# Lightning attention into a gated FFN: the first score matmuls of block n+2 moved behind the state update of block n+1

## The chip, the cores and the metric

The kernel runs on one core of a Trainium2 chip. The time is the device time of one execution in microseconds, over several runs; a separate execution is recorded by the profiler.

## What is computed

Two stages, one behind the other, on q, k, v of 4 batches, 8 heads, 768 positions and 64 features:

```python
# stage 1: linear attention with decay lam per head, block after block
intra = (qb @ kb.T * Dmask) @ vb            # within a block, lower triangle, lam ** (i - j)
inter = (qb * lam_pow) @ kv_state           # what earlier blocks left
out[block] = intra + inter
kv_state = lam_block * kv_state + (kb * rev_pow).T @ vb
# stage 2: x = out as (3072 tokens, 512), d_ff = 1536
y = (sigmoid(x @ w_gate) * (x @ w_val)) @ w_out
```

## The kernel before, in words

The sequence is cut into six blocks of 128 positions (`C = 128`, twice the reference's block; the decays are made for 128). Block n holds 128 positions of each of the four batches, so 512 tokens for the FFN. The order of the instructions on every engine is the order in which the program writes them (`tc.manual_schedule`): nothing is reordered, and each engine and each issuing queue goes through its own list.

For one block the pieces are:

- `load(n, "qkv", 0, B)` (L70 to L93): GpSimd (POOL) issues the loads of Q, K and V, cast to bf16.
- `transpose_by_dma(n)` (L225): SyncE (SP) issues two DMA transposes, Q into `QR` and K into `KR`, two buffers each. They wait for the loads.
- `t(n, bp)` (L268, `scale`, L242): VectorE (DVE) multiplies `QR` of a pair of batches by the decay into `QS`.
- `sc(n, bp)` and `m(n, bp)`: for each of the pair's two batches 8 score matmuls into two PSUM tiles `sp` (L299), and the masking multiplications `MT` on VectorE (L204), two for each batch.
- `a(n, 0, 1)` (`piece_a`, L316): 32 matmuls of `QS` with the state `Sb` (L324) and 32 of `MT` with V (L312) into four PSUM tiles `op`, one for each pair `bp` and `u`; four casts carry these into `XT[n]` (L339), the FFN's input.
- `c(n, 0, 1)` (L399): 32 matmuls of V with the decayed K (`kd`, made by POOL, L373) into two PSUM tiles `cp`; VectorE adds the faded old state `sd` (L382) into `Sb` (L406).
- `gv(n, ft)` (L410): 4 gate matmuls (`gp`, L415), a sigmoid on ScalarE (ACT, L418), 4 value matmuls (`vp`, L421), and the product `ht` on VectorE (L424), for each of 12 slices of d_ff.
- `piece_po(n, tt)` (L475): 12 matmuls with `WO` (L478), a copy on ScalarE (L481), and a store issued by SP (L486), for each of the four batches.

PSUM has eight buffers: five (`ps_at`, tag `ps`) go round among `op`, `sp` and the first `cp`; three (`ps_ff`, tag `ff`) go round among `gp`, `vp`, `po` and the second `cp`.

The loop from L638 on weaves block n's FFN with block nx = n+1's attention. In block n come, in this order: the transposes of nx; slices 0 and 1; fade, decayed K and the loads of n+2; slices 2 to 8; the scale of nx's first pair; slice 9; the scale of its second pair; slice 10; the scores of the first pair; slice 11; their second mask; then output matmuls of batch 0, scores of the second pair, outputs of batches 1 and 2, `a(nx)`, `c(nx)`, and outputs of batch 3. Ahead of the loop (L621 to L637) the same is written out for block 1's FFN and block 2's attention. Matmuls of the FFN use the whole 128\*128 array; the scores use it as 64\*128, `a` as 64\*64 and then 128\*64, and `c` as 128\*64.

Of the kernel before, what the change touches and what calls it, by code (L numbers as in the profile page):

```python
# [15 lines left out]
def kernel(  # L16
# [11 lines left out]
    nc = tc.nc  # L28
# [3 lines left out]
    NSTEP = S // C  # L32
# [144 lines left out]
    mask = const.tile([128, H, C], FP32, tag="mask")  # L177
# [22 lines left out]
    def masked(out, x, n, u):  # L200
        if n == 0:
            nc.vector.tensor_tensor(out=out, in0=x, in1=mask[:, u::2, :], op=ALU.mult)  # L202
            return
        nc.vector.tensor_tensor(  # L204
            out=out.rearrange("p (e x) c -> p e x c", e=2), in0=x.rearrange("p (e x) c -> p e x c", e=2),
            in1=mask.rearrange("p (x u e) c -> p u e x c", u=2, e=2)[:, u], op=ALU.mult)

    def half(e):
        return slice(e * 64, (e + 1) * 64)

    def head(g, u):
        return 4 * (g % 2) + 2 * u + g // 2
# [12 lines left out]
    def transpose_by_dma(n):  # L225
        QR[n] = trsb.tile([128, 2, B, 2, C], BF16, tag="QR", name="QR", bufs=2)
        kt = trsb.tile([128, 2, B, 2, C], BF16, tag="KR", name="KR", bufs=2)
        for dst, src in ((QR[n], Q[n]), (kt, K[n])):
            nc.sync.dma_start_transpose(out=dst.rearrange("p e b x c -> p (e b x) c"),
                                        in_=src.rearrange("p e b y d -> p (e b y d)"))  # L230
        for bp in range(NB2):
            KS[n, bp] = kt[:, :, 2 * bp:2 * bp + 2]
# [35 lines left out]
    def piece_t(n, bp):  # L268
        if n > 1 or bp == 1:
            scale(n, bp, QR[n][:, :, 2 * bp:2 * bp + 2] if n > 1 else HB["q"])  # L270
            return
        q1, k1 = (x[1][:, 0].rearrange("p (e b y d) -> p e b y d", e=2, b=2, y=HP) for x in (Q, K))
        tq = ps_at.tile([128, 2, 2, 2, C], BF16, name="tq", tag="ps")
        tk = ps_at.tile([128, 2, 2, 2, C], BF16, name="tk", tag="ps")

        def turn(out, x):
            for e in range(2):
                for i in range(2):
                    for g in range(2):
                        nc.tensor.transpose(out[:, e, i, g, :],  # L280
                                            x[:, e, i, 2 * g:2 * g + 2, :].rearrange("p y d -> p (y d)"), ident)

        turn(tq, q1)
        scale(n, bp, tq)
        turn(tk, k1)
        KS[n, bp] = trsb.tile([128, 2, 2, 2, C], BF16, tag="KS", name="KS")
        nc.scalar.copy(KS[n, bp], tk)
# [16 lines left out]
    def piece_m(n, b, us=(0, 1)):  # L304
        if us[0] == 0:
            MT[n, b] = mtp.tile([128, 2, HP, C], BF16, tag="MT", name="MT")
        for u in us:
            masked(MT[n, b][:, u], SP[n, b][u], n, u)

    def intra(n, b, out, m, start, stop):  # L310
        for e in range(2):
            nc.tensor.matmul(out[half(e)], lhsT=V[n][:, b, 2 * m + e, :],  # L312
                             rhs=MT[n, b][:, e, m, :] if n == 0 else MT[n, b][:, m % 2, 2 * e + m // 2, :],
                             start=start, stop=stop, skip_group_check=True)

    def piece_a(n, pairs):  # L316
        OP = {(bp, u): ps_at.tile([128, 2, 2, C], FP32, name="op", tag="ps")
              for bp in pairs for u in range(2)}
        for bp in pairs:
            for i in range(2):  # L320
                for x in range(2):
                    for u in range(2):
                        for e in range(2):
                            nc.tensor.matmul(OP[bp, u][half(e), x, i, :],  # L324
                                             lhsT=Sb[half(u), 2 * bp + i, 2 * e + x, :],
                                             rhs=QS[n, bp][half(u), e, i, x, :],
                                             start=(i == 0 and x == 0), stop=False,
                                             skip_group_check=True)
        for bp in pairs:
            for u in range(2):  # L330
                for i in range(2):
                    for x in range(2):
                        intra(n, 2 * bp + i, OP[bp, u][:, x, i, :], 2 * x + u, False, i == 1 and x == 1)
        if n not in XT:
            XT[n] = xtp.tile([128, NMT, B, C], BF16, tag="XT", name="XT")
        for bp in pairs:
            for u in range(2):
                cp = nc.vector.tensor_copy if n == 1 and bp == 0 and u else nc.scalar.copy
                cp(XT[n][:, u::2, 2 * bp:2 * bp + 2, :], OP[bp, u])  # L339

    def piece_a0(b, split=False):
# [44 lines left out]
    def kdh(n, b, h):  # L386
        if n == 1:
            return KD[n][:, b // 2].rearrange("p (e b y d) -> p e b y d", e=2, b=2, y=HP)[:, h % 2, b % 2, h // 2]
        return KD[n][:, b, h, :] if n == 0 else KD[n][:, h % 2, b, h // 2, :]

    def c(n, *pairs):
        for bp in pairs:
            pool, tag = (ps_at, "ps") if bp == 0 or n == 0 else (ps_ff, "ff")
            cp = pool.tile([128, 2, HP, D], FP32, name="cp", tag=tag)
            for i in range(2):
                for hp in range(HP):
                    for u in range(2):
                        h = head(hp, u)
                        nc.tensor.matmul(cp[half(u), i, hp, :], lhsT=kdh(n, 2 * bp + i, h),  # L399
                                         rhs=V[n][:, 2 * bp + i, h, :], start=(i == 0 and hp == 0),  # L400
                                         stop=(i == 1 and hp == HP - 1), skip_group_check=True)
            dst = Sb[:, 2 * bp:2 * bp + 2]
            if n == 0:
                nc.vector.tensor_copy(dst, cp)
            else:
                nc.vector.tensor_tensor(out=dst, in0=cp, in1=SD.pop(bp), op=ALU.add)  # L406
# [68 lines left out]
    def piece_po(n, tt):  # L475
        po = ps_ff.tile([128, DM], FP32, name="po", tag="ff")
        for ft in range(NFT):
            nc.tensor.matmul(po, lhsT=HT[n, ft][:, tt * 128:(tt + 1) * 128],  # L478
                             rhs=WO[:, ft, :], start=(ft == 0), stop=(ft == NFT - 1))
        ob = osb.tile([128, DM], FP32, tag="ob", name="ob")  # L480
        nc.scalar.copy(ob, po)  # L481
        parts = 2 if n == 0 and tt < 2 else 1
        rows = 128 // parts
        for i in range(parts):
            lo = tt * S + n * C + i * rows
            nc.sync.dma_start(out=out[lo:lo + rows, :], in_=ob[i * rows:(i + 1) * rows, :])  # L486
# [51 lines left out]
    def t(n, bp):  # L538
        piece_t(n, bp)

    def sc(n, bp):
        piece_s(n, [2 * bp, 2 * bp + 1])
        piece_m(n, 2 * bp)

    def m(n, bp):
        piece_m(n, 2 * bp + 1)

    def a(n, *pairs):
        piece_a(n, pairs)

    def gv(n, *fts):
        for ft in fts:
            piece_gv(n, ft)
# [39 lines left out]
    t(1, 0)  # L593
    gv(0, 9)
    sc(1, 0)
    m(1, 0)
    gv(0, 10)
# [11 lines left out]
    t(1, 1)  # L609
    gvh(1, 0, 6, 7)  # L610
    sc(1, 1)
    gvh(1, 0, 8)
    m(1, 1)
# [12 lines left out]
    t(2, 1)  # L626
    piece_po(0, 3)
    sc(2, 0)
    m(2, 0)
    piece_po(1, 0)  # L630
    sc(2, 1)
    m(2, 1)
    piece_po(1, 1)
    piece_po(1, 2)
    a(2, 0, 1)
    c(2, 0, 1)
    piece_po(1, 3)  # L637
    for n in range(2, NSTEP):  # L638
        nx = n + 1
        if nx == NSTEP:  # L640
            gv(n, *range(NFT))
            for tt in range(B - 1):
                piece_po(n, tt)
            piece_last(n, B - 1)
            break
        transpose_by_dma(nx)
        gv(n, 0, 1)
        if nx + 1 < NSTEP:
            fade()
            make_kd(nx)  # L650
            load(nx + 1, "qkv", 0, B)
        gv(n, 2, 3, 4, 5, 6, 7, 8)
        t(nx, 0)
        gv(n, 9)
        t(nx, 1)
        gv(n, 10)
        sc(nx, 0)
        gv(n, 11)
        m(nx, 0)
        piece_po(n, 0)  # L660
        sc(nx, 1)
        m(nx, 1)
        piece_po(n, 1)
        piece_po(n, 2)
        a(nx, 0, 1)
        if nx + 1 < NSTEP:
            c(nx, 0, 1)
        piece_po(n, 3)


# [28 lines left out]
```

## Time and profile before

| | |
|---|---|
| median of 3 runs | 226.52 us (226.45 to 226.9) |
| profiled execution | 226.60 us, of which the profiled span is 224.5 us |
| granted TensorE clock | 1.000 |
| TensorE matmuls busy | 218.5 us (97% of the span) |
| VectorE / ScalarE / GpSimd busy | 105.5 / 79.6 / 78.4 us |
| one block in the loop | 34.6 us (first gate matmul of blocks 2 and 3 at 87.1 and 121.7 us) |

The profile names an instruction by engine, line and tiles: "PE sp L299" is a score matmul. PE is TensorE's matmuls, PEld its weight loads; a row "sp<-QS,KR x16" is a group of 16. A time in a list of the timeline is the start from the beginning of the span, followed by the length. In the chain of work that ended last, a row starts where the one before it ends. Matmuls are pipelined and their ends are modelled, so the distance of two starts is the safer measure.

### The profile page before, as it was taken

How to read it: one execution, taken by the hardware profiler on the slowest of the kernel's cores; microseconds unless marked ns; L12 is line 12 of the kernel's file. 1: busy time of each engine (PE TensorE's matmuls, PEld its weight loads, DVE VectorE, ACT ScalarE, POOL GpSimd, SP SyncE). 2: the span in 40 equal slices, each digit the busy share in tenths (PEclk: the TensorE clock that was granted, in tenths of full speed). 3: DMA queues.
4: the chain of work that ended last, by engine and by line, in shares of the span. 5: the costliest groups of instructions: out<-in, count | busy, mean ns of one | idle time of the engine just before them, and what ended most of it. 6: DMA issues, size and time to landing. Idle time of an engine off the chain costs nothing.

```text
span 224.5 us, 4265 instructions
## 1 busy us (share of the span) xinstructions
PE 218.5 (97%) x1748; PEld 114.6 (51%) x1748; DVE 105.5 (47%) x192; ACT 79.6 (35%) x150; POOL 78.4 (35%) x77
## 2 busy tenths in 40 slices
PE   7799999999999999999999999999999999999994
PEld 2454455888854454444445444446444445444443
DVE  7796847595530713336732445742335840333300
ACT  5664334435422234333225333115333225333221
POOL 8995698983691008930006940000000000000000
PEclk9999999999999999999999999999999999999999
DMA  6999999999999992999021999021920012100022
GB/s 109 155 173 194 189 176 156 157 194 166 157 198 184 217 178 83 204 156 108 1 96 55 230 145 133 1 96 47 176 62 0 0 53 91 47 3 0 0 93 95
DMA packets 105891, 25.70 MB, mean 114 GB/s; under 512 B 96016, under 2 KB 102928, under 8 KB 105872
## 3 DMA queue, kind: packets, MB, share of 16 engines
q0 software_dynamic: 81264, 13.90, 80.0%
q1 hardware_dynamic: 23568, 11.28, 19.7%
q10 hardware_dynamic: 1040, 0.26, 0.5%
q8 instruction: 13, 0.21, 0.4%
q14 instruction: 6, 0.05, 0.1%
HBM read 28.32 MB, written 6.29 MB: 154 GB/s over the span
## 4 chain that ended last, share of the span: by engine, by line
PE 94%; DMA 3%; DVE 1%; issue 1%; ACT 1%; POOLq 0%
PE po L478 27%; PE gp L415 21%; PE vp L421 21%; PE gp L450 5%; PE gp L429 5%; PE vp L456 5%; PE op L312 3%; PE sp L299 3%; DMA kb<-in_k_dram 3%; PE op L324 1%; PE cp L399 1%; PE po L467 1%; DVE MT L202 1%; PE tk L238 0%; ACT XT L352 0%
## 5 line engine op out<-in xcount | busy, mean ns | idle before, releaser
L424 DVE TENSOR_TENSOR ht<-sg,vp 128x512 bf16<-128x512 bf16 x54 | 37.1, 687 | 64.0 <-PE vp L421 63.9
L478 PE MATMUL po<-WO,ht 128*128 128x512 bf16 x276 | 62.0, 380 | 0.0
L415 PE MATMUL gp<-XT,WG 128*128 128x512 bf16 x216 | 55.5, 380 | 0.0
L421 PE MATMUL vp<-XT,WV 128*128 128x512 bf16 x216 | 55.4, 379 | 0.0
L418 ACT ACTIVATE sg<-gp 128x512 bf16<-128x512 f32 x54 | 32.2, 597 | 59.0 <-PE gp L415 59.0
L478 PEld LDWEIGHTS <-ht 128*128 128x128 bf16 x276 | 26.3, 98 | 31.0
L421 PEld LDWEIGHTS <-WV 128*128 128x128 bf16 x216 | 21.1, 98 | 25.5
L415 PEld LDWEIGHTS <-WG 128*128 128x128 bf16 x216 | 20.8, 98 | 24.7
L481 ACT COPY ob<-po 128x512 f32<-128x512 f32 x23 | 13.5, 585 | 52.3 <-PE po L478 50.4
L204 DVE TENSOR_TENSOR MT<-sp,mask 128x512 bf16<-128x512 f32 x40 | 25.2, 683 | 10.1 <-PE sp L299 10.1
L382 POOL TENSOR_TENSOR sd<-Sb,dec 128x512 f32<-128x512 bf16 x8 | 8.1, 1037 | 42.0 <-DVE Sb L406 42.0
L450 PE MATMUL gp<-XT,WG 128*128 128x256 bf16 x96 | 14.4, 273 | 0.0
L456 PE MATMUL vp<-XT,WV 128*128 128x256 bf16 x96 | 14.4, 273 | 0.0
L460 DVE TENSOR_TENSOR ht<-sg,vp 128x256 bf16<-128x256 bf16 x24 | 10.0, 420 | 8.6 <-PE vp L456 8.6
L453 ACT ACTIVATE sg<-gp 128x256 bf16<-128x256 f32 x24 | 9.2, 383 | 13.0 <-PE gp L450 11.9
L91 POOL DMA_DIRECT2D vb<-in_v_dram x10 | 12.8, 1281 | 0.8 <-DMA WG<-in_moe_w_gate_dram 0.6
L373 POOL TENSOR_TENSOR kd<-kb,kds 128x1024 bf16<-128x1024 bf16 x6 | 11.3, 1904 | 4.1 <-DMA kb<-in_k_dram 4.1
L406 DVE TENSOR_TENSOR Sb<-cp,sd 128x512 bf16<-128x512 f32 x8 | 5.2, 686 | 15.4 <-PE cp L399 15.4
L339 ACT CAST XT<-op 128x512 bf16<-128x512 f32 x19 | 9.9, 598 | 2.1 <-PE op L312 2.0
L450 PEld LDWEIGHTS <-WG 128*128 128x128 bf16 x96 | 9.2, 98 | 1.8 <-issue 0.2
L456 PEld LDWEIGHTS <-WV 128*128 128x128 bf16 x96 | 9.4, 98 | 1.1
L77 POOL DMA_DIRECT2D qb<-in_q_dram x8 | 9.4, 1184 | 0.0
(79 smaller groups left out, 161.7 us busy)
## 6 DMA issues: line engine op xcount, KB each, us to landing
out_dram<-ob SPq DMA_DIRECT2D x21, 256.0 KB, 2.1
kb<-in_k_dram POOLq DMA_DIRECT2D x10, 256.0 KB, 8.7
qb<-in_q_dram POOLq DMA_DIRECT2D x8, 256.0 KB, 8.3
vb<-in_v_dram POOLq DMA_DIRECT2D x4, 512.0 KB, 13.2
WO<-in_moe_w_out_dram POOLq DMA_DIRECT2D x3, 512.0 KB, 8.6
WG<-in_moe_w_gate_dram POOLq DMA_DIRECT2D x5, 256.0 KB, 8.5
WV<-in_moe_w_val_dram POOLq DMA_DIRECT2D x5, 256.0 KB, 9.0
qb<-in_q_dram POOLq DMA_DIRECT2D x6, 128.0 KB, 8.3
```

The costliest lines, as they stand in the source:

```text
L91: nc.gpsimd.dma_start(out=lst[n][:, b0:b1], in_=src[b0:b1, :, sl, :].rearrange("b h s d -> s (b h) d"))
L204: nc.vector.tensor_tensor(out=out.rearrange("p (e x) c -> p e x c", e=2), in0=x.rearrange("p (e x) c -> p e x c", e=2), in1=mask.rearrange ...
L373: nc.gpsimd.tensor_tensor(out=KD[n][:, e], in0=K[n][:, e], in1=kds[:, e::2].unsqueeze(1).unsqueeze(3).to_broadcast([128, B, HP, D]), op=AL ...
L415: nc.tensor.matmul(gp, lhsT=WG[:, mt, fs], rhs=x[:, mt, :], start=(mt == 0), stop=(mt == NMT - 1))
L418: nc.scalar.activation(sg, gp, AF.Sigmoid)
L421: nc.tensor.matmul(vp, lhsT=WV[:, mt, fs], rhs=x[:, mt, :], start=(mt == 0), stop=(mt == NMT - 1))
L424: nc.vector.tensor_mul(HT[n, ft], sg, vp)
L429: nc.tensor.matmul(ps[:, lo:hi], lhsT=W[:, mt, ft * 128:(ft + 1) * 128], rhs=x[:, mt, lo:hi], start=(mt == 0), stop=(mt == NMT - 1))
L450: nc.tensor.matmul(gp[:, cs], lhsT=WG[:, mt, fs], rhs=x[:, mt, cs], start=(mt == 0), stop=(mt == NMT - 1))
L456: nc.tensor.matmul(vp[:, cs], lhsT=WV[:, mt, fs], rhs=x[:, mt, cs], start=(mt == 0), stop=(mt == NMT - 1))
L478: nc.tensor.matmul(po, lhsT=HT[n, ft][:, tt * 128:(tt + 1) * 128], rhs=WO[:, ft, :], start=(ft == 0), stop=(ft == NFT - 1))
L481: nc.scalar.copy(ob, po)
```

## The change

The scores of the first pair of batches (batches 0 and 1) of block n+2 are computed in block n, directly behind the state update `c` of block n+1, where they stood inside the next block's gate/value slices. What feeds them moves ahead with them: the two DMA transposes of block n+2 are issued behind slice 11 of block n in program order, and the scale of its first pair runs between the outputs of batches 1 and 2. Ahead of the loop the same is done for block 3. The scale of the second pair keeps its block and stands behind slice 8. The casts of `op` into `XT` with u = 1 go to VectorE for all blocks from 2 on; they were on ScalarE.

```diff
@@ piece_a
-                cp = nc.vector.tensor_copy if n == 1 and bp == 0 and u else nc.scalar.copy
+                cp = nc.vector.tensor_copy if u and (n > 1 or bp == 0) else nc.scalar.copy
                 cp(XT[n][:, u::2, 2 * bp:2 * bp + 2, :], OP[bp, u])
@@ ahead of the loop
     m(2, 0)
+    transpose_by_dma(3)
     piece_po(1, 0)
     sc(2, 1)
     m(2, 1)
     piece_po(1, 1)
+    t(3, 0)
     piece_po(1, 2)
     a(2, 0, 1)
     c(2, 0, 1)
+    sc(3, 0)
+    m(3, 0)
     piece_po(1, 3)
     for n in range(2, NSTEP):
         nx = n + 1
...
-        transpose_by_dma(nx)
+        more = nx + 1 < NSTEP
         gv(n, 0, 1)
-        if nx + 1 < NSTEP:
+        if more:
             fade()
             make_kd(nx)
             load(nx + 1, "qkv", 0, B)
         gv(n, 2, 3, 4, 5, 6, 7, 8)
-        t(nx, 0)
-        gv(n, 9)
         t(nx, 1)
-        gv(n, 10)
-        sc(nx, 0)
-        gv(n, 11)
-        m(nx, 0)
+        gv(n, 9, 10, 11)
+        if more:
+            transpose_by_dma(nx + 1)
         piece_po(n, 0)
         sc(nx, 1)
         m(nx, 1)
         piece_po(n, 1)
+        if more:
+            t(nx + 1, 0)
         piece_po(n, 2)
         a(nx, 0, 1)
-        if nx + 1 < NSTEP:
+        if more:
             c(nx, 0, 1)
+            sc(nx + 1, 0)
+            m(nx + 1, 0)
         piece_po(n, 3)
```

`sc` gets a switch `mask` as well, which leaves its first mask out; no call uses it.

More of the change, by code (lines that the diff above doesn't have):

```diff
@@ L539, in t, with sc @@
         piece_t(n, bp)
-    def sc(n, bp):
+    def sc(n, bp, mask=True):
         piece_s(n, [2 * bp, 2 * bp + 1])
-        piece_m(n, 2 * bp)
+        if mask:
+            piece_m(n, 2 * bp)
     def m(n, bp):
```

## The prediction

> **What bounds the kernel now.** I read the page first: busy time by engine, then the slices.
>
> ```profile
> PE 218.5 (97%) x1748; PEld 114.6 (51%) x1748; DVE 105.5 (47%) x192; ACT 79.6 (35%) x150; POOL 78.4 (35%) x77
> PE   7799999999999999999999999999999999999994
> PEclk9999999999999999999999999999999999999999
> ```
>
> TensorE (PE) is full from about 10 us to the end, at the full clock; VectorE (DVE) and ScalarE (ACT) work less than half of the time. So an edit is worth what it does to TensorE's own stream: time that it takes out of it, or waits that it puts in. Next the chain that ended last, for one block (104 to 123 us), columns start, length, instructions:
>
> ```profile
> 105.40 0.86 PE vp L421 x4
> 106.26 0.55 PE sp L299 x16
> 106.81 0.97 PE gp L415 x4
> ...
> 117.08 0.57 PE op L324 x32
> 117.65 1.01 PE op L312 x32
> 118.66 0.50 PE cp L399 x32
> 119.16 2.70 PE po L478 x12
> ```
>
> The chain is TensorE alone, without a wait. Look at the four-matmul groups: 0.86 us in a row of their kind, 0.97 behind the scores (sp). The timeline agrees start by start: last vp 105.88, first sp 106.19, so 0.31 where vp follows vp in 0.216; last sp 106.60, next gp 106.75, 0.15 where pairs of sp follow in 0.054. Each time the shape used of the array changes (128\*128, 64\*128, 64\*64, 128\*64), some 0.09 to 0.1 us go. From op L312 to cp L399, both 128\*64, it costs nothing: 118.44 to 118.49, the ordinary pitch.
>
> Third, who empties PSUM behind the attention (timelines of ACT and DVE; the DVE cast is the one instance of that form, in block 1):
>
> ```profile
> 118.03 2.05 ACT L339 CAST XT<-op 128x512 bf16<-128x512 f32 x4 [0.33 <-PE op L312]
> 119.02 1.29 DVE L406 TENSOR_TENSOR Sb<-cp,sd 128x512 bf16<-128x512 f32 x2 [4.94 <-PE cp L399]
> 38.63 0.69 DVE L339 CAST XT<-op 128x512 bf16<-128x512 f32 x1 [0.42 <-PE op L312]
> ```
>
> Four casts occupy ACT to 120.08, and nobody on TensorE waits for them now. Last, SP's queue of issues:
>
> ```profile
> 57.08 4.96 SPq L229 DMA_TRANSPOSE QR<-qb  x1
> 62.13 3.58 SPq L229 DMA_TRANSPOSE KR<-kb  x1
> 66.27 22.02 SPq L486 DMA_DIRECT2D out_dram<-ob  x10
> 88.39 1.77 SPq L229 DMA_TRANSPOSE QR<-qb  x1
> 90.26 1.76 SPq L229 DMA_TRANSPOSE KR<-kb  x1
> ```
>
> A transpose that is issued while loads fill the DMA engines (57 to 66 us) holds SP for 3.6 to 5.0 us instead of 1.8, and by the tile views it lands 8.9 us after its issue. The others: QR 3.8, 3.8 and 5.1; KR 6.0 and 7.9 (loads start behind it) and 4.9 (no load after it).
>
> **What the Trainium skill says.** "TensorEngine Tiling (Array Packing)", Key Properties: "Changing tiling mode (not just tile) drains the TensorE". The trace agrees, 0.09 to 0.1 us each; the page gives no price. The same page, PSUM Bottleneck, says that tiling hastens TensorE but not the emptying of PSUM, and to use ScalarE and VectorE for it. That is what the new split of casts does; whether it is enough is worked out below. "DMA: Bandwidth & Descriptors", Queues, rings and completion order: each DMA engine goes round-robin, packet by packet, between its queues. The 8.9 us landings under load fit that.
>
> **The change, part by part.** The sum is against the profiled execution: 226.60 us, of which 224.5 are the span and 2.1 lie around it. The runs' median is 226.52, 0.08 less.
>
> 1\. *Scores out of the gate/value stretch.* Three blocks are concerned: scores of blocks 3, 4 and 5, batches 0 and 1. Removed each time: 0.55 (sp) and the 0.11 by which the next gp is longer (0.97 less 0.86), so 0.66. Put back behind cp L399: 16 matmuls with an entry from 128\*64 to 64\*128. That step does not occur in the trace; the nearest are L324 to L312 (117.43 to 117.58, 0.15 for a pitch of 0.054) and L399 to po (118.97 to 119.10, 0.13 for 0.03), so 0.09 to 0.1 again, and sp costs its 0.55. The po behind it is long already (2.70 for 2.59, since it follows cp), and stays so behind sp. Saved: 0.11 per block, **0.33 in all**. Bounds: 0 if that step is dear, 0.6 (three times 0.2) if it is free.
>
> 2\. *PSUM.* All of op, cp and sp share five buffers. Behind sc(nx, 1) come four op, one cp and four sp, so the four new sp take exactly the buffers of the four op, in order: OP(0,0), OP(0,1), OP(1,0), OP(1,1). The first scores have to wait until the casts have emptied them. Before, the next user of these buffers came much later. In the clock of the block shown, the last intra matmuls of the four start at 117.77, 117.99, 118.22 and 118.44 and end 0.22 later. ACT now casts OP(0,0) from 118.03 to 118.61 and OP(1,0) from 118.51 to 119.10. DVE casts OP(0,1) from about 118.28, takes 0.69, and follows with OP(1,1) 0.60 later (the pitch of its pairs: 1.29 for two of 0.69), so 118.88 to 119.57. TensorE reaches the first batch at 119.09 (all free) and the second at 119.31; its second matmul wants OP(1,1) and goes at 119.57 + 0.05 (what passes between the end of ACT's KS copy and the score matmul that waits for it, at 8.8 us) = 119.62. **Wait: 0.3 us**, I take 0.34 with the semaphore step that DVE shows ahead of such a read. It stands in each of three blocks. Had ACT kept all four casts, the last would end at 120.08 and the wait would be 0.8. Bounds: 0.1 if DVE starts and releases as fast as ACT, 0.5 if it is later.
>
> 3\. *DVE behind it.* After the casts: two state adds (1.29) and the four masks (2.48) that formerly lay between the ht products. From 119.5 that ends at about 123.2. The first ht of the next block needs vp at about 124.3 (121.86 plus two groups of 0.86, plus 0.55 and 0.34). Cover 1.1 us: nothing. If it were gone, ht would be late, and TensorE would wait for a gate buffer two groups on. In the gate/value stretch DVE gets the same instructions back as room; DVE idles 1.04 ahead of each ht there. The fade on POOL waits for the state add, some 0.5 us later than now, and moves the loads behind it; they land over 10 us before use. ACT loses two casts, nothing waits for it.
>
> 4\. *Transposes a block ahead, in the loop.* SP meets them behind the store of po(n-1, 3), waits for the load of Q and K of block n+2 (K by 103 in this block, from POOL issues at 93 to 94 us plus landings of 8.5), and issues at once, while V is still coming (to 106). With 5.0 + 8.9 us, KR has landed by 117 at worst, about 112 more likely. SP is past both before the store of po(n, 0) at 111.9. The scale of t(nx+1, 0), 0.68 on DVE, runs at 114, behind the masks of sc(nx, 1), and the scores come at 119. Hidden; the moved scale takes the place of one before ht 9. In the next block V ends at 141 and the scores come at 154. Cost nothing.
>
> 5\. *Transposes of block 3, ahead of the loop.* Here the cover is thin. They stand behind the store of po(0, 3), issued at 74.04 to 74.38. Block 3's second K load was issued at 65.4 and took 12.3 (77.7), its V load at 66.5 took 15.2 (81.7): the DMA engines are full. QR(3) goes at 74.4; KR(3) at 77.7 if SP is free, at 79.4 if QR holds SP for 5.0 as at 57.08. The scale of t(3, 0) waits for QR(3) with the casts of XT(2) and both state adds queued behind it on DVE, and TensorE waits for those casts by part 2. QR lands at 79 to 83.3; with 83.3 the scale ends at 84.0 and the casts at 85.3, against 84.7 wanted. The scores want KR(3) at 84.5 on TensorE, with po(1, 3) and the whole next stretch behind them. KR lands at 77.7 + 4.9 = 82.6 at best and at 79.4 + 8.9 = 88.3 at worst. I take 79.4 + 5.5, since V is gone at about 82 and no load follows until 91: 84.9. **Wait 0.5 us**, once, with the 0.34 of this block inside it; bounds 0.2 and 3.8. The store of po(1, 0) moves from 77.3 to some 83, which nobody waits for with four ob buffers.
>
> Sum: 226.60 - 0.33 + 2 x 0.34 + 0.5 = 227.45, or **227.4** on the median's scale.
>
> **Rivals.** A measurement of this kernel can tell 0.2% (0.45 us) from no change; the runs lie within 226.45 to 226.9.
>
> *A, the forecast*: the PSUM wait outweighs the saved change of shape and block 3's KR is a little late: 226.9 to 228.2. For it: the five buffers, and the 57 to 71 us transposes. Chance 0.46.
>
> *B, not slower*: the array saving survives. Place: the second batch of scores behind cp. It decides at a wait of 0.11 per block: if DVE empties OP(1,1) by 119.4 (casts nearer 0.5 than 0.69), and KR(3) is there at 84.5, the sum is -0.33 + 3 x 0.1, down to -0.33: 226.2 to 226.5. With half of the waits, up to 226.9. Against it: the one DVE cast took 0.69. Chance 0.30, nearly all of it within 0.2%.
>
> *C, late transposes*: QR(3) and KR(3) share the engines with K and V and hold each other up, KR at 87 to 88.3 and DVE's casts late as well: +2.5 to +3.8 in place of 0.5, so 229.4 to 230.7. For it: both landings of 8.9. Against it: the loads end at 82. Chance 0.20.
>
> *D, faster by over 0.2%*: needs over 0.45, while the two changes of shape per block that can go at most are worth 0.6, with no wait at all. Chance 0.04.
>
> The numbers: the range 226.2 to 229.0 takes in A and B and the lower edge of C. Faster 0.04, same 0.29, slower 0.67.
>
> **What would show it.** In the changed profile: gp groups at 0.86 throughout the stretch where sp stood; sp L299 directly behind cp L399; a gap of about 0.3 inside those 16 matmuls, ended by the DVE cast L339, in blocks 2 and 3 (part 2); the casts of u = 1 on DVE, 0.69 each; QR(3) and KR(3) issued at 74 to 79 us and TensorE waiting for KR or for the scale at 84.5 to 85 (part 5); loop transposes issued near 100 and 135 us, with no wait (part 4). I am wrong if the sp behind cp run through without a gap, if block 3's wait is over 1.5 us, or if DVE's masks push the first ht late.

## The result, and the profile after

The changed kernel takes 233.38 us (median of 6 runs, 232.84 to 234.53) against 226.57 before: a ratio of 1.0301, 95% interval 1.0275 to 1.0327. It is slower by 6.8 us where 0.9 was forecast and 229.0 was the upper end. The profiled execution took 233.75 us with a span of 232.0, and its mean TensorE clock was 0.984.

The page of the changed kernel, busy time and slices of TensorE and its clock (in tenths):

```profile
PE 221.0 (95%) x1748; PEld 115.7 (50%) x1748; DVE 110.2 (48%) x200; ACT 75.7 (33%) x142; POOL 78.5 (34%) x77
PE   7699999999999966999999999999999999999995
PEclk9999999999999995899999999999999999999999
```

The loss stands in two neighbouring slices, 81 to 93 us, once: the prologue's last stretch, not the loop. And the clock has a hole that begins in the second of them. Before, both rows were unbroken there. The list of waits names the first half of the loss (us in all, times, longest), and the stretches (columns: stretch, its length, busy us of PE, PEld, DVE, ACT and POOL with counts, granted clock, DMA share, GB/s) the second:

```profile
PE sp L299 <- DMA KR<-kb: 4.2, 1, 4.2
```

```profile
80.00:84.70 4.70, 4.70 (x106) 2.88 (x105) 0.00 (x0) 2.05 (x4) 0.00 (x0) 1.00 1.55 165
84.70:89.10 4.40, 0.26 (x17) 0.14 (x10) 3.08 (x5) 0.20 (x1) 0.75 (x1) 0.86 1.11 275
89.10:94.70 5.60, 5.56 (x27) 2.41 (x28) 2.48 (x4) 0.00 (x0) 5.60 (x5) 0.50 0.01 5
94.70:100.00 5.30, 5.30 (x26) 2.45 (x25) 1.37 (x2) 2.33 (x4) 5.30 (x5) 1.00 1.23 120
```

TensorE stands still from the end of the state update to 89.1 us, and then works 5.6 us at half its clock. Its timeline shows what that costs:

```profile
84.29 0.67 PE L399 MATMUL cp<-vb,kd 128*64 128x64 bf16 x32
89.14 1.04 PE L299 MATMUL sp<-QS,KR 64*128 64x128 bf16 x16 [4.18 <-DMA KR<-kb]
90.11 5.00 PE L478 MATMUL po<-WO,ht 128*128 128x512 bf16 x12
```

Twelve output matmuls take 5.00 us where 2.7 to 2.8 are usual (start to start 0.427 us in place of 0.216). SP's queue shows why KR is late:

```profile
74.87 5.10 SPq L229 DMA_TRANSPOSE QR<-qb  x1
80.08 5.44 SPq L229 DMA_TRANSPOSE KR<-kb  x1
```

Each transpose of block 3 holds SP over 5 us. QR lands at 85.75 and KR at 89.09, 10.9 and 9.0 us after their issues. V's load landed 15.2 us after its issue in the kernel before; now it takes 18.6 (to 85.6 us). VectorE shows the queue behind the scale that waits for QR:

```profile
85.78 0.69 DVE L242 TENSOR_TENSOR QS<-QR,lamq 128x1024 bf16<-128x1024 bf16 x1 [5.90 <-DMA QR<-qb]
86.39 1.28 DVE L339 CAST XT<-op 128x512 bf16<-128x512 f32 x2
87.58 1.28 DVE L406 TENSOR_TENSOR Sb<-cp,sd 128x512 bf16<-128x512 f32 x2
```

The casts that empty the `op` tiles end at 87.67 only. So a second wait is hidden behind the one for KR: the scores need those PSUM buffers. Even with KR there in time TensorE would have waited for them, by an estimate from these rows some 2.6 us (from 85.1, where the second batch of scores would have stood, to 87.7).

In the loop the picture is the forecast one. The gate groups of block 2 all take 0.86 us, and the casts now stand in its chain:

```profile
124.25 0.57 PE op L324 x32
124.82 0.59 PE op L312 x16
125.41 0.02 issue
125.43 1.30 DVE XT L339 x2
126.73 0.04 issue
126.77 0.38 PE sp L299 x7
127.15 2.69 PE po L478 x12
```

The chain leaves TensorE for VectorE's two casts and comes back to the scores: a wait on PSUM that was not there before.

**The account.** I measure from the first output matmul of block 0 (po) to the last matmul of the kernel, which leaves out the loads at the start: 158.57 us before, 165.66 after, so 7.09 more. It is the wait for KR, 4.25 (first sp at 89.14 where 84.89 was due); the half clock, 2.64 (0.3 on the 16 scores, 2.34 on the output matmuls); the saved change of shape, three times -0.11; and the PSUM wait, two times 0.26 (the third is inside the KR wait). Sum 7.1. This is the profiled execution; how the other five divide between wait and clock no trace shows.

### The profile page after: what moved, and what is told of

Read it like the earlier page. It is cut to its first block, busy times and chain, and to the rows that moved or that the text cites. A ratio compares the mean times of both kernels' runs of the same rounds, so it can differ in the third digit from the quotient of the medians.

```text
span 232.0 us, 4271 instructions
## 1 busy us (share of the span) xinstructions
PE 221.0 (95%) x1748; PEld 115.7 (50%) x1748; DVE 110.2 (48%) x200; ACT 75.7 (33%) x142; POOL 78.5 (34%) x77
## 4 chain that ended last, share of the span: by engine, by line
PE 86%; DMA 7%; SPq 2%; DVE 2%; issue 1%; ACT 1%; POOLq 0%
PE po L478 24%; PE gp L415 20%; PE vp L421 20%; PE gp L450 5%; PE gp L429 5%; PE vp L456 5%; DMA KR<-kb 4%; DMA kb<-in_k_dram 3%; PE sp L299 2%; SPq L229 2%; PE op L312 2%; PE po L467 1%; DVE XT L339 1%; PE op L324 1%; DVE MT L202 1%
## 5 line engine op out<-in xcount | busy, mean ns | idle before, releaser
L478 PE MATMUL po<-WO,ht 128*128 128x512 bf16 x276 | 64.2, 389 | 0.0
L478 PEld LDWEIGHTS <-ht 128*128 128x128 bf16 x276 | 26.8, 100 | 32.8 <-issue 3.0
L339 DVE CAST XT<-op 128x512 bf16<-128x512 f32 x9 | 5.8, 685 | 11.8 <-PE op L312 11.8
L299 PE MATMUL sp<-QS,KR 64*128 64x128 bf16 x128 | 5.8, 229 | 4.3 <-DMA KR<-kb 4.2
L242 DVE TENSOR_TENSOR QS<-QR,lamq 128x1024 bf16<-128x1024 bf16 x8 | 5.4, 684 | 8.8 <-DMA QR<-qb 8.8
```

## The experiments

The kernel before was run again beside each group of experiments, with medians of 226.55 to 226.56 us; the ratios of the experiments are against these runs. The column "chain" is the distance just defined, from each kernel's one profiled execution.

| kernel | median us | ratio, 95% interval | chain us | against before |
|---|---|---|---|---|
| before | 226.57 | | 158.57 | |
| changed | 233.38 | 1.0301 [1.0275, 1.0327] | 165.66 | +7.09 |
| fill_wait | 232.27 | 1.0245 [1.0212, 1.0278] | 164.61 | +6.04 |
| po_first | 229.78 | 1.0127 [1.0081, 1.0173] | 160.45 | +1.88 |
| v_later | 226.77 | 1.0016 [1.0006, 1.0025] | 159.03 | +0.46 |
| scores_back | 227.75 | 1.0045 [1.0026, 1.0063] | 159.35 | +0.79 |
| loop_only | 226.74 | 1.0007 [0.9996, 1.0017] | 158.88 | +0.31 |
| loop_act | 227.99 | 1.0054 [1.0035, 1.0073] | 159.96 | +1.39 |
| v_later_ff | 226.24 | 0.9983 [0.9974, 0.9991] | 158.44 | -0.12 |
| before_v_later | 226.57 | 0.9999 [0.9987, 1.0011] | 158.57 | 0.00 |
| trans_ahead | 226.58 | 1.0006 [0.9995, 1.0017] | 158.56 | 0.00 |
| casts_only | 226.33 | 0.9986 [0.9976, 0.9997] | 158.57 | 0.00 |

**fill_wait: is the slow stretch the price of standing idle?**

```diff
+    wf = psum()
+    for i in range(20):
+        nc.tensor.matmul(wf, lhsT=zero[:, :C], rhs=zero, start=True, stop=True, skip_group_check=True)
     sc(3, 0)
```

> 20 idle 128x512 matmuls of zeros (4.3 us at full clock) stand between the state update and the scores of block 3, where the changed kernel waits 4.3 us for KR. Theory 'the clock falls because TensorE stood idle over 4 us': the clock stays at 1.0, the output matmuls behind keep their pitch of 0.216 us, and the time is 226.6 + 4.3 (fill in place of the wait) - 0.33 + 0.42 + 0.1 = 231.1 us. Rival 'the slow matmuls behind the wait have another cause (late ht, weight loads, the stores)': they stay at 0.43 us and the time stays at 233.4 us.

TensorE's timeline (the fill writes a tile that bears the name gp):

```profile
84.40 4.49 PE L642 MATMUL gp<-zero 128*128 128x512 bf16 x20
90.23 0.62 PE L299 MATMUL sp<-QS,KR 64*128 64x128 bf16 x16 [1.35 <-DMA KR<-kb]
90.79 2.76 PE L478 MATMUL po<-WO,ht 128*128 128x512 bf16 x12
```

The clock stays at 1.000 (0.998 to 1.000 in all four runs, against 0.984 to 0.993 in the six of the changed kernel), and the twelve output matmuls are back at 2.76 us, though the scores started a full us later than in the changed kernel. So the slow stretch belongs to the idling, as "TensorE: Matmul & The Clock Gate" of the Trainium skill has it (Part 1, What's actually happening: the clock is halved after an idle window of about 3.4 us and given back after a busy one). The changed kernel agrees in kind, with other lengths. Its stretches show where the clock fell:

```profile
84.80:87.80 3.00, 0.16 (x10) 0.04 (x4) 2.02 (x4) 0.10 (x1) 0.00 (x0) 1.00 1.22 266
87.80:88.80 1.00, 0.00 (x0) 0.00 (x0) 1.00 (x2) 0.00 (x0) 0.45 (x1) 0.52 1.03 387
```

The last matmul ahead of the wait starts at 84.76 and the clock falls at 87.8, 3.1 us later; it is back at 94.7, 5.5 us after the scores set in. Nor is 3.1 us a fixed length: at the ends of the profiled executions, where no matmul follows, the recorded falls come from 2.3 us (changed kernel, po_first) to 5.1 us (loop_only) after the start of the last one. The time of fill_wait is 1.2 above the expectation since KR landed later here, at 90.2, and left 1.4 to wait behind the fill: 20 x 0.216 + 1.41 + 2 x 0.155 = 6.04, the measured chain (0.155 is what a moved block costs in the loop, some 0.26 of wait less 0.11 saved).

**po_first: the same wait, partly filled with work.** The last output matmuls of block 1 go ahead of `sc(3, 0)` and `m(3, 0)`.

> The last output matmuls of block 1 go ahead of the scores of block 3, so 2.6 us of the wait for KR are filled with work. Theory 'a wait below some 3 us keeps the clock': the scores wait about 1.7 us, clock 1.0, time 226.6 + 1.7 + 0.42 - 0.22 = 228.5 us. Rival 'any wait of a us or more slows the clock behind it': 230.8 us, that is only the 2.6 us less than the changed kernel's 233.4.

In the profile:

```profile
85.09 2.76 PE L478 MATMUL po<-WO,ht 128*128 128x512 bf16 x12
89.36 0.62 PE L299 MATMUL sp<-QS,KR 64*128 64x128 bf16 x16 [1.50 <-DMA KR<-kb]
89.91 1.04 PE L415 MATMUL gp<-XT,WG 128*128 128x512 bf16 x4
```

This run has a wait of 1.5 us, no slow stretch and 228.79 us, as the first theory says. But the four runs spread over 228.72, 228.79, 230.77 and 232.73 (the ratio in the table is over the first three), and the latter two have mean clocks of 0.993 and 0.985 against 0.998 and 1.000. By an estimate from these means the clock was halved for 3.2 and 6.9 us there, which is 1.6 and 3.5 of the 2.0 and 4.0 us that they took longer. So this kernel did not keep the clock in every run; how long the wait was in those two no trace shows.

**v_later: is it V's load that delays the transposes?**

```diff
-    load(3, "qkv", 0, B)
+    load(3, "qk", 0, B)
...
             make_kd(nx)
+            if n == 2:
+                load(3, "v", 0, B)
             load(nx + 1, "qkv", 0, B)
```

> The load of V of block 3 is issued one stretch later (behind the decayed K of block 3, about 91 us), so that no load runs beside the two transposes of block 3 once K has landed at 78 us. Theory 'the transposes share the DMA engines packet by packet with V, and both are slower for it': KR(3) lands at about 84.5 us in place of 89.1, TensorE waits 0 to 0.5 us, clock 1.0, time 226.8 to 227.5 us. Rival 'the issue itself is slow at that place: SP is held 5 us by each transpose whatever the loads do': KR lands at 88 to 89 and the time is 232.5 to 233.4 us.

SP's queue:

```profile
74.69 4.71 SPq L229 DMA_TRANSPOSE QR<-qb  x1
80.08 1.71 SPq L229 DMA_TRANSPOSE KR<-kb  x1
```

QR, under K's load (which ended at 80.0), still holds SP for 4.7 us. KR, with no load beside it, holds it 1.7 us and lands 3.9 after its issue, at 83.98. TensorE does not wait for it, the clock is 1.000, and 6.6 us of the loss are gone; the 0.46 that are left are three times 0.155. KR was issued at the same 80.08 as in the changed kernel, and the edit moves V's load alone. That settles that V's load makes KR late. How the two hinder each other is seen in the DMA packets of the changed kernel (columns: packets, MB, time of the packets as a share of 16 engines): in 3 us (80 to 83) the transposes' queue (q1) and the loads' queue (q0) move

```profile
q1 hardware_dynamic: 1235, 0.32, 79.8%
q0 software_dynamic: 1233, 0.16, 79.6%
```

packets, one for one, as the round robin would have it; but together 2468, where in equally long stretches loads alone move 3685 (101 to 104 us of the changed kernel) and transposes alone 3350 (90 to 93 us of the kernel before):

```profile
q0 software_dynamic: 3685, 0.47, 244.5%
```

```profile
q1 hardware_dynamic: 3350, 0.85, 124.9%
```

Side by side they move 26 to 33% fewer packets than either does alone. A transpose's packet is twice as large, so in bytes the two together move as much as the loads alone (0.47 MB), where transposes alone move 0.85. Besides, a transpose starts late behind running loads. QR of block 4 was issued at 102.31 in the changed kernel, and from 102.4 to 106.4 its queue has no packet at all:

```profile
q0 software_dynamic: 4860, 0.62, 244.9%
```

Its first packet moves 4.4 us after its issue, QR of block 3's 4.7 us after; without loads beside it (QR at 88.39 in the kernel before) it is 1.3 us. So of the 10 to 11 us that these two take to land, over 4 pass before anything is shared, which the round robin does not tell of. Why is not shown, for the late start as for the lower rate.

**scores_back: does the early transpose do harm without the early scores?** `sc(3, 0)` and `m(3, 0)` go back to their place around slice 11 of block 2.

> Transposes and first scale of block 3 stay early as in the changed kernel, but its first scores go back between slices 10 and 11 of block 2. Theory 'the direct wait of the scores for KR(3) is nearly all of the loss': no wait for KR, but the casts of XT(2) on VectorE stand behind the scale that waits for QR(3) (85.8 us) and end at 87.7, so the first gate matmul of block 2 waits 0.5 us: 226.6 + 0.5 - 0.22 + 0.42 = 227.3 us. Rival 'the early transposes do the harm in other ways too (stores, loads of block 4, VectorE's order)': 229 us or more.

The gate did wait about half a us, as expected, but at another instruction:

```profile
88.34 1.02 PE L421 MATMUL vp<-XT,WV 128*128 128x512 bf16 x4 [0.32 <-DVE Sb L406]
```

The first gate matmuls had their XT in time. The first value matmuls wanted the buffer of the second cp, which the state add frees, queued on VectorE behind the scale that waited for QR: 0.48 in the starts. With two loop blocks at 0.155 each that makes 0.79, the whole of the chain's difference. So in this profile the transposes harm in one other way alone, VectorE's order. It is one of the three shortest runs, though (227.04 to 227.19); the other five took 227.67 to 228.21 at the same clock, and what they lost more no trace shows.

**loop_only and loop_act: the PSUM wait.** Block 3 as before the change, blocks 4 and 5 as changed; loop_act keeps all casts on ScalarE.

> Blocks 4 and 5 as in the changed kernel, block 3 as before the change (its transposes at the head of block 2, its first scores between slices 10 and 11). Theory 'in the loop the moved scores cost 0.21 of PSUM wait and save 0.11 per block': 226.55 - 2 x 0.11 + 2 x 0.21 = 226.75 us, no wait for KR, clock 1.0. Rival 'transposes that are issued under the loads cost something in the loop as well': 227.5 us or more.

> As loop_only, but all casts of XT of blocks 2 and up stay on ScalarE. Theory 'the second scores wait for the last cast of op': the last cast ends 0.5 us later than with two engines, so the wait is 0.7 us in place of 0.21 in each of two blocks and the time is 1.0 us above loop_only, 227.7 us. Rival 'the wait of 0.21 is a fixed cost of changing the array's shape': no difference to loop_only, 226.75 us.

loop_only is +0.31 on the chain: 2 x 0.155. Its runs cannot tell it from before (interval 0.9996 to 1.0017). That its median meets the expected 226.75 is partly luck: the wait was 0.26 and not 0.21, and the time around the span is 0.33 shorter than before (see the controls). loop_act is 1.08 above it on the chain and 1.25 in the medians, for 1.0 expected; a wait of 0.8 per block by the starts (0.32 ahead of the ninth score, 0.48 ahead of the tenth), now for ScalarE:

```profile
119.69 0.76 PE L299 MATMUL sp<-QS,KR 64*128 64x128 bf16 x9
120.73 0.38 PE L299 MATMUL sp<-QS,KR 64*128 64x128 bf16 x7 [0.28 <-ACT XT L339]
```

So the wait depends on who casts the op tiles, and when: it is no cost of the array's shape.

**v_later_ff: the wait taken away.** In v_later the fourth of the moved score tiles comes from the FFN's buffers.

```diff
-            sp = [pool.tile([128, HP, C], FP32, name=f"sp{u}", tag=tag) for u in range(2)]
+            own = last if b == bs[-1] and last else (pool, tag)
+            sp = [pool.tile([128, HP, C], FP32, name="sp0", tag=tag),
+                  own[0].tile([128, HP, C], FP32, name="sp1", tag=own[1])]
...
-            sc(nx + 1, 0)
+            sc(nx + 1, 0, last=(ps_ff, "ff"))
```

> As v_later, but the fourth of the moved score tiles (second batch, u = 1) takes one of the three FFN buffers, so that it does not wait for the cast of the last op. Theory 'the wait of 0.21 is for that one buffer, and 0.11 per block is really saved': the gap inside the 16 score matmuls goes, and the time is 226.55 - 0.33 = 226.2 us, 0.6 below v_later (226.77). Rival 'the FFN buffer is then late itself': TensorE waits ahead of the first gate or value matmul of the next block, 226.7 us or more.

The 16 scores of block 2, first in v_later and then here:

```profile
119.23 0.88 PE L299 MATMUL sp<-QS,KR 64*128 64x128 bf16 x16
```

```profile
118.95 0.62 PE L301 MATMUL sp<-QS,KR 64*128 64x128 bf16 x16
```

The gap of 0.26 is gone. A block takes 34.55 us, 34.75 in v_later and 34.59 before. The rival is right in a small way: the first value matmul of each block now comes 0.07 late (0.284 behind the last gate matmul, in place of 0.216). Net -0.04 per block, -0.12 in all. The median shows -0.32, more than the chain explains; see the next two.

**before_v_later, trans_ahead, casts_only: controls.**

> The kernel before the change, with V of block 3 loaded one stretch later as in v_later. It shows what that move does alone: 226.55 us, no difference, if no one waits for loads at that place; below 226.4 if V's load already cost something before the change.

> The kernel before, with only the DMA transposes of blocks 4 and 5 issued a block ahead as in the changed kernel; scores, scales and casts stand where they stood. Theory 'transposes under the loads are hidden in the loop': TensorE's chain is unchanged, span 224.5 us. What lies around the span, 2.12 us before and 1.78 in each kernel that has any of the loop's changes, is open: if it is 1.8 here, the order on SP's queue brings it; if 2.1, the moved scores or scales do.

> The kernel before, with only the casts of u = 1 on VectorE. Theory: nobody waits for the casts there, so the time is unchanged, 226.55 us. Rival 'VectorE's two extra casts delay the state update or ht': 226.8 us or more. What lies around the span should stay at 2.12 us, since the changed loop with all casts on ScalarE has 1.77 too.

None changes the chain. V's move gains nothing by itself, and the loop's transposes under the loads are hidden. But casts_only is 0.22 faster by the runs. What lies around the span in the profiled executions is 2.11 us before and in trans_ahead, 2.10 in before_v_later, 1.89 in casts_only, and 1.77 to 1.80 in every kernel with moved scores. My expectation of 2.12 for casts_only failed. So some 0.2 to 0.34 us outside of the profiled span go with the program, whatever the stage gains; what they are stays open. v_later_ff beats both kernels by the runs (0.9983), but only 0.12 of it is shown to come from this schedule.

## Why the prediction was wrong

The direction was forecast, and both waits were named. But what forecast A rested on, the PSUM wait against the saved change of shape, makes 0.2 us of the 7.1 (0.52 less 0.33). The rest came in the way that had been given to rival C at a chance of 0.20, and by a term that no rival had.

- **Part 5, the transposes of block 3**, is the step that failed: "I take 79.4 + 5.5, since V is gone at about 82". KR was issued at 80.08, near enough, and landed 9.0 later, beyond the stated worst of 88.3. The mistake is in the reason given: V is not gone at 82 when transposes run beside it, it ends at 85.6. The row that I had read as the bound (8.9 for KR at 62 us) was the right one to take for a place with the same traffic; for QR even its own row (8.9) was too short, since it took 10.9 and landed at 85.75 where 83.3 was the latest allowed for. "Wait 0.5 us" measured 4.25, past the 1.5 that was named as a sign of being wrong.
- **A term was missing.** Rival C foresaw late transposes at +2.5 to +3.8, but had the price of a wait as its length. This one was long enough to halve the clock (2.64 us, put at nothing), and 4.25 us of wait cost 6.9. That put the result beyond C's 230.7 as well.
- **Part 2, PSUM**: which buffer, which cast and who waits were right. 0.34 was 0.26, so 0.08 too dear, about half of it the semaphore step that I had added on top. The 0.8 with ScalarE alone is what loop_act shows.
- **Part 1**: 0.11 per block was right, and v_later_ff shows it: 34.59 to 34.55 with 0.07 of new wait.
- **Part 3**: right in the loop. VectorE still idles 1.38 ahead of the first ht of block 3, for a cover of 1.1; the prediction's own terms for that vp add up to 124.5, not 124.3.
- **Part 4**: right in its cost; trans_ahead shows it. The room is to be read in v_later, where block 3 is not late: KR(4) holds SP to 112.8, past the 111.9 at which SP was to be free for the store of po(2, 0), and lands at 114.9, where 112 was called likely and 117 the worst. The store goes out at 112.9, and nobody waits for it; the scores come at 119.2.
- **Rival B**: v_later reaches its number (226.77, where B ends at 226.9), but not by its mechanism. Its chain is 0.46 longer than before, and the time around the span happens to be 0.33 shorter. The saving survives as B has it in v_later_ff alone.

## What to carry to other kernels

When a transfer is moved earlier, price it by the row that ran in the same traffic, and count what it does to the transfers beside it: their ends move too. A stall of TensorE that lasts until its clock falls costs more than its length (here 6.9 us for 4.25). The falls on record came 2.3 to 5.1 us after the last matmul's start, so fill such a stall or keep it well below that. Scores behind a state update save a change of shape (0.11 us), which one PSUM buffer freed by a late cast more than takes back (0.26).

## What the runs showed that I had not expected

Transposes and loads in flight together moved 2468 packets in 3 us, against 3685 or 3350 alone. A transpose issued under such loads held SP for up to 6.9 us (KR of block 4 in v_later), in place of 1.7 to 1.8; but the hold does not tell the landing, for QR of block 4 in the changed kernel held SP for 1.4 us and landed 10.0 after its issue. And the time outside of the profiled span changed by up to 0.34 us between kernels whose TensorE chains agree within 0.01 us or differ for known reasons, which is as much as the 0.33 that this change was to gain.
